# First pair's keys in two loads of 64 and 192 tiles instead of three, and the queries' load written with a leading dimension of two

## The chip, the cores and the metric

The kernel runs on one core of one Trainium2 chip. The metric is the device time of one execution in microseconds; a median of several runs is given, and one further execution was taken with the hardware profiler. Names of engines: PE is TensorE (PEld its weight loads), DVE is VectorE, ACT is ScalarE, POOL is GpSimd, SP is SyncE, which here only issues loads.

## The reference

One step of attention decoding with grouped queries: 32 query heads share 8 key and value heads, the context is 65,536 long, a head has 128 elements, all in bf16.

```python
B, Hq, Hkv, Sq, Sk, D = 1, 32, 8, 1, 65536, 128
...
k = jnp.repeat(k, rep, axis=1)
v = jnp.repeat(v, rep, axis=1)
scale = D ** -0.5
scores = jnp.einsum("bhqd,bhkd->bhqk", q, k) * scale
p = _softmax(scores, axis=-1)
return jnp.einsum("bhqk,bhkd->bhqd", p, v)
```

Keys and values are 134.2 MB each and are read once.

## The kernel before

Each of the 8 heads' context is cut into two halves, which makes 16 pairs of units ("pairs"). A pair has 256 tiles; a tile is 128 keys (one per partition) by 128 elements, so a pair's keys are 64 KB in each of the 128 partitions, and its values as many. The buffer `kbuf` holds a pair and 96 tiles more, `vbuf` one pair.

**TensorE** runs one loop over the pairs (`tensor_engine`, L223). Before the keys of pair i it takes the values of pair i-1 (`pe_values`). In the first round there are none, and it transposes the queries instead (`pe_queries`, L217): it waits for `q_sem`, which the queries' load raises, and for the identity matrix, makes one transpose at L220, and waits until DVE has copied the result. Then come the keys (`pe_keys`, L164): groups of eight tiles are transposed into PSUM (`pe_transposes`, the matmul at L139), evicted to `ktb` by DVE (L245) or ACT (L243), and multiplied with the head's queries (`pe_scores`, L157) eight groups later. The first 20 groups (160 tiles) form the first unit of the pair, the last 12 (96 tiles) the second. The code of the last 12 groups stands twice, behind an If each, for even and odd pairs.

**What the keys' loads promise.** `K_PARTS = (0, 64, 160)` gives the tiles at which TensorE takes a semaphore: `krdy[0]` ahead of tile 0, `krdy[1]` ahead of tile 64 (group 8), `krdy[2]` ahead of tile 152 (group 19, the last of the first unit). `load_k(i, odd, split)` makes one load for each entry of `split`: a load that begins at part f and reaches to the next entry raises `krdy[f]` by 16 when it has landed, and the semaphores of the parts that it swallows are raised by SP itself, right after the issue. Most pairs are loaded in one piece, the first in three.

**SP** (`sync_engine`, L457) issues, in this order: pair 0's keys, pair 0's values, then for every further pair its keys after `kfree` and its values after `vfree`. `kfree` is raised by DVE and ACT when the group 19 of the pair before is in PSUM (L241), `vfree` by DVE when the pair's value products are done (L326). All these loads run on one queue, in the order of issue. The last pair's values come in pieces, so that little work is left when the last has landed.

**ACT** issues the queries' load as its first instruction (L428): 32 rows of 128 elements into 32 partitions. It is on ACT's own queue, beside the keys.

DVE, ACT and POOL also make the softmax: maxima, exponentials and their sums for a unit of 160 and one of 96 tiles, and the rescaling of the running output.

Of the kernel before, what the change touches and what calls it, by code (L numbers as in the profile page):

```python
# [41 lines left out]
def take(e, sem, n=1):  # L42

    e.wait_ge(sem, n)
    e.sem_inc(sem, -n)  # L45


def bass_standalone__gqa_softmax__decode_kernel(nc, q, k, v, out):
# [14 lines left out]
    def row_tile(odd, x):  # L63
        return (x + C) % (2 * T) if odd else x

    kf, vf, qf, of = k[0], v[0], q[0, :, 0, :], out[0, :, 0, :]
# [4 lines left out]
    def sb(name, shape, dt):  # L71
        return S(nc.sbuf_tensor(name, shape, dt))

    def sem(name):
        return S(nc.semaphore(name))
# [5 lines left out]
    qsb = sb("qsb", [HR, D], DT.bfloat16)  # L81
# [42 lines left out]
    q_sem, o_sem, s_x, t_z, t_id, t_if, t_qT = (  # L124
        sem(n) for n in ("q_sem", "o_sem", "s_x", "t_z", "t_id", "t_if", "t_qT"))
# [294 lines left out]
    def act_round(e, i):  # L420
        for j in range(G):
            if on_act(j):
                evict(e, j)
        exponentials(e, 2 * i)
        exponentials(e, 2 * i + 1)

    def scalar_engine(e):
        e.dma_start(qsb[:, :], qf).then_inc(q_sem, 16)  # L428
        e.wait_ge(t_z, 1)
        e.activation(dscr[:, 1:2], dscr[:, 0:1], AF.Exp, scale=1.0)  # L430
        with e.Fori(0, H):
            for i in range(HALVES):
                act_round(e, i)
        e.wait_ge(t_row, 1)
        e.dma_start(of[0:HR - R, :], orow[R:HR, :]).then_inc(o_sem, 16)
# [17 lines left out]
    def pairs(x):  # L453

        return x.rearrange("h (c p t) d -> (h c) p (t d)", c=HALVES, p=P)

    def sync_engine(e):  # L457
        kp, vp = pairs(kf), pairs(vf)

        def cols(a, b):  # L460
            return slice(a * D, b * D)

        def load_k(i, odd, split=(0,)):

            for n, f in enumerate(split):
                last = (split + (len(K_PARTS),))[n + 1]
                a, b = K_PARTS[f], (K_PARTS + (2 * T,))[last]
                r = row_tile(odd, a) if b - a < 2 * T else 0
                t = r if odd else C + r
                e.dma_start(kbuf[:, cols(t, t + b - a)], kp[i][:, cols(r, r + b - a)]).then_inc(krdy[f], 16)  # L470
                for x in range(f + 1, last):
                    e.sem_inc(krdy[x], 16)

        def load_v(i, ready, a, b):
            e.dma_start(vbuf[:, cols(a, b)], vp[i][:, cols(a, b)]).then_inc(ready, 16)

        def load_both(i, odd):
            take(e, kfree)
            load_k(i, odd)
            take(e, vfree)  # L480
            load_v(i, vrdy[0], 0, 2 * T)
            e.sem_inc(vrdy[1], 16)

        load_k(0, 0, (0, 1, 2))
        load_v(0, vrdy[0], 0, 2 * T)

        for sm in [vrdy[1]] + vpiece:
            e.sem_inc(sm, 16)
        load_both(1, 1)
        with e.Fori(1, H - 1) as h:  # L490
            load_both(2 * h, 0)
            load_both(2 * h + 1, 1)
        i = NR - 2
        take(e, kfree)
        load_k(i, 0, (0, 2))
        take(e, vfree)
        load_v(i, vrdy[0], 0, A)
        load_v(i, vrdy[1], A, 2 * T)
        i = NR - 1
        take(e, kfree)  # L500
        load_k(i, 1, (0, 1, 2))
        take(e, vfree)
        for sm in vpiece:
            e.sem_inc(sm, -16)
        load_v(i, vrdy[0], C, 2 * T)
        e.sem_inc(vrdy[1], 16)
        r = 0
        for n, sm in zip(V_PIECES, vpiece):
            load_v(i, sm, r, r + n)
            r += n  # L510
        ins = e.dma_start(of[HR - R:HR, :], olast[:, :])
        ins.wait_op(t_last, 1, "sem-ge")
        ins.then_inc(o_sem, 16)


    tensor_engine(nc.tensor)
    vector_engine(nc.vector)
    scalar_engine(nc.scalar)
    gpsimd_engine(nc.gpsimd)
    sync_engine(nc.sync)  # L520
    nc.sync.wait_ge(o_sem, 32)
    es.close()
# [27 lines left out]
```

## Time and profile before

| | us |
|---|---|
| median of 3 runs (lowest, highest) | 628.41 (628.28, 628.63) |
| span of the profiled execution | 627.2 |
| PE busy | 489.5 (78%) |
| DVE busy | 284.8 (45%) |
| ACT busy | 235.2 (37%) |
| q1, SP's queue: data moved | 268.44 MB |
| rate over the span | 428 GB/s |

The span runs from the first to the last instruction of the profiled execution; the runs' times also hold what lies around it. In the page's rows of forty slices, one slice is 15.7 us, and each digit is a busy share in tenths. "DMA" there is the mean over the core's 16 DMA engines. A row of the timeline gives start, duration, engine, line, operation, what is written and what read, the count, and in brackets how long the engine was idle before and what ended that; "issue" means that the profile shows nothing it waited for. A row of a DMA queue gives packets, MB and the packets' time as a share of 16 engines over the window; the packets of a short window are put to the window in which they begin, so a share there can be over 100%. Queue q1 is SP's, q10 ACT's, and q8 brings instructions. A load's row of packets consists of one packet per partition and a small one of 4 bytes per engine that reports the end.

### The profile page before, as it was taken

To read this page: it belongs to the slowest core of one execution; us is meant where nothing else is said; L and a number is where in the kernel's file an instruction comes from. 1 tells how busy PE (TensorE), PEld (TensorE's weight loads), DVE (VectorE), ACT (ScalarE), POOL (GpSimd) and SP (SyncE) were. 2 spreads that over 40 slices of the span, in tenths; PEclk is the share of its full clock that TensorE was granted. 3 is DMA by queue.
4 is the path that set the end of the run, shared out by engine and by line. 5 is a ranking of instruction groups with operands and counts; after the bars stand their busy time and mean duration, and the time that the engine had idled before them with its cause. 6 is when DMAs were issued, how large, how long until landed. Compare 5 with 4: busy or idle time off the path is not lost. (4 is left out here: it accounts for less than half of the span.)

```text
span 627.2 us, 27059 instructions
## 1 busy us (share of the span) xinstructions
PE 489.5 (78%) x12290; PEld 485.2 (77%) x12290; DVE 284.8 (45%) x667; ACT 235.2 (37%) x466; POOL 16.4 (3%) x49
## 2 busy tenths in 40 slices
PE   1773995949959497696976949779595896999897
PEld 1773995949859497696976949779595896989896
DVE  2531553615536164351644516345172452747264
ACT  1430442504425053251533605335152351535253
POOL 0000000000000000000000000000000000000000
PEclk9975886958869597685977959779596785969596
DMA  9999999999999999999999999999999999999997
GB/s 366 441 442 431 435 435 430 439 430 439 418 447 418 447 422 435 435 430 435 435 435 430 439 422 443 426 439 426 443 426 443 422 447 422 423 428 429 427 439 308
DMA packets 6155, 268.59 MB, mean 428 GB/s; under 512 B 770, under 2 KB 898, under 8 KB 1154
## 3 DMA queue, kind: packets, MB, share of 16 engines
q1 hardware_dynamic: 6056, 268.44, 99.2%
q8 instruction: 7, 0.11, 0.1%
q10 hardware_dynamic: 90, 0.02, 0.0%
q14 instruction: 2, 0.02, 0.0%
HBM read 268.44 MB, written 0.01 MB: 428 GB/s over the span
## 5 line engine op out<-in xcount | busy, mean ns | idle before, releaser
L139 PE MATMUL trb<-ident,kbuf 128*128 128x128 bf16 x4096 | 302.7, 237 | 107.0 <-PEq L45 100.4
L139 PEld LDWEIGHTS trb<-ident,kbuf 128*128 128x128 bf16 x4096 | 270.8, 107 | 108.5 <-issue 108.2
L243 ACT ACTIVATE ktb<-trb 128x1024 bf16<-128x1024 bf16 x176 | 180.1, 1023 | 350.6 <-PE trb L139 344.2
L245 DVE COPY ktb<-trb 128x1024 bf16<-128x1024 bf16 x336 | 222.0, 689 | 167.1 <-PE trb L139 164.0
L157 PE MATMUL qkb<-qcur,ktb 128*128 128x4 bf16 x4096 | 132.0, 164 | 0.0
L157 PEld LDWEIGHTS qkb<-qcur,ktb 128*128 128x128 bf16 x4096 | 124.1, 96 | 0.0
L183 PE MATMUL pvb<-pts,vbuf 128*128 128x4 bf16 x2560 | 71.6, 165 | 12.7 <-PEq L45 12.7
L183 PEld LDWEIGHTS pvb<-pts,vbuf 128*128 128x128 bf16 x2560 | 69.8, 101 | 14.6 <-issue 14.6
L413 ACT ACTIVATE pts<-qkb,negm 128x160 bf16<-128x160 f32 (+1 forms) x128 | 51.9, 548 | 0.0
L280 DVE TENSOR_REDUCE cmax<-qkb 128x4 f32<-128x640 f32 (+1 forms) x32 | 22.1, 691 | 59.6 <-DVEq L45 59.6
L183 PE MATMUL qkb<-pts,vbuf 128*128 128x4 bf16 x1536 | 43.3, 166 | 4.6 <-PEq L45 4.6
L183 PEld LDWEIGHTS qkb<-pts,vbuf 128*128 128x128 bf16 x1536 | 42.4, 104 | 5.1 <-issue 5.0
L413 ACT ACTIVATION_READ_ACCUMULATOR pts<-qkb,negm 128x1 f32 x128 | 34.2, 267 | 0.0
L449 POOL PARTITION_ALL_REDUCE cmaxa<-cmax x32 | 12.0, 374 | 576.5 <-POOLq L45 576.5
L407 ACT ACTIVATE alpha<-dm 128x4 f32<-128x4 f32 x32 | 6.4, 201 | 32.0 <-ACTq L45 32.0
L330 DVE COPY acc<-qkb 128x4 f32<-128x4 f32 x8 | 1.3, 162 | 35.2 <-DVEq L45 35.2
L308 DVE TENSOR_TENSOR lp<-lp,alpha 128x4 f32<-128x4 f32 x24 | 3.9, 163 | 26.9 <-DVEq L45 26.9
L319 DVE TENSOR_TENSOR acc<-acc,pvb 128x4 f32<-128x4 f32 x32 | 5.1, 158 | 22.6 <-DVEq L45 21.8
L220 PE MATMUL trb<-ident,qsb 32*128 32x32 bf16 x1 | 0.2, 178 | 11.7 <-issue 11.7
L220 PEld LDWEIGHTS trb<-ident,qsb 32*128 32x128 bf16 x1 | 0.1, 100 | 11.6 <-issue 11.6
L297 DVE TENSOR_TENSOR m<-m,cmaxa 128x4 f32<-128x4 f32 x24 | 3.8, 160 | 8.8 <-DVEq L45 8.8
L316 DVE TENSOR_TENSOR acc<-acc,alpha 128x4 f32<-128x4 f32 x24 | 3.9, 162 | 4.2 <-DVEq L45 3.7
(42 smaller groups left out, 37.6 us busy)
## 6 DMA issues: line engine op xcount, KB each, us to landing
kbuf<-in_k_dram SPq DMA_DIRECT2D x5, 3072.0 KB, 24.6
vbuf<-in_v_dram SPq DMA_DIRECT2D x2, 5120.0 KB, 23.2
kbuf<-in_k_dram SPq DMA_DIRECT2D x1, 5120.0 KB, 17.8
kbuf<-in_k_dram SPq DMA_DIRECT2D x2, 2048.0 KB, 13.4
vbuf<-in_v_dram SPq DMA_DIRECT2D x1, 3072.0 KB, 26.9
vbuf<-in_v_dram SPq DMA_DIRECT2D x1, 1984.0 KB, 30.8
vbuf<-in_v_dram SPq DMA_DIRECT2D x1, 704.0 KB, 32.1
vbuf<-in_v_dram SPq DMA_DIRECT2D x1, 288.0 KB, 32.4
```

Source lines behind the costliest of these rows:

```text
L139: ins = pe.transpose(trb[j % NTB][:, i * P:(i + 1) * P], kbuf[:, t * D:(t + 1) * D], ident[:, :])
L157: ins = pe.matmul(bank[:, t * R:(t + 1) * R], lhsT=ktb[:, off:off + P], rhs=qcur[:, :], start=True, stop=True)
L183: ins = pe.matmul(vsum[q], lhsT=vbuf[:, r * D:(r + 1) * D], rhs=pts[:, r * R:(r + 1) * R], start=r == a, stop=r == b - 1)
L243: ins = e.activation(dst, trb[j % NTB][:, :], AF.Copy).then_inc(eva, 1)
L245: ins = e.tensor_copy(dst, trb[j % NTB][:, :]).then_inc(evd, 1)
L280: e.tensor_reduce(cmax[:, :], qkb[part][:, 0:n * R].rearrange("p (t g) -> p g t", g=R), AX.X, ALU.max).then_inc(cm, 1)
L308: chain(e, lambda: e.tensor_tensor(lp[:, :], lp[:, :], alpha[u % 2][:, :], ALU.mult), lambda: e.tensor_tensor(lp[:, :], lp[:, :], rsum[u % ...
L316: return lambda: e.tensor_tensor(acc, acc, alpha[u % 2][:, :], ALU.mult)
L319: return lambda: e.tensor_tensor(acc, acc, vsum[q], ALU.add)
L407: e.activation(alpha[u % 2][:, :], dm[u % 2][:, :], AF.Exp, scale=scale)
L413: ins = e.activation(pv[:, g, r:r + n], sv[:, g, 0:n], AF.Exp, bias=negm[b][:, g:g + 1], scale=scale, accum_out=rsum[b][:, g:g + 1])
L449: e.partition_all_reduce(cmaxa[:, :], cmax[:, :], P, bass.bass_isa.ReduceOp.max).then_inc(cma, 1)
```

## The change

```diff
     def scalar_engine(e):
-        e.dma_start(qsb[:, :], qf).then_inc(q_sem, 16)
+        e.dma_start(qsb[:, :], qf.rearrange("(a b) d -> a b d", a=2)).then_inc(q_sem, 16)
...
-        load_k(0, 0, (0, 1, 2))
+        load_k(0, 0, (0, 1))
         load_v(0, vrdy[0], 0, 2 * T)
```

The first pair's keys are loaded in two pieces: tiles 0 to 63 as before, and tiles 64 to 255 in one load, which raises `krdy[1]`; SP raises `krdy[2]` itself behind it. The queries' source is written as two blocks of 16 rows.

On SP, at the start of the program, the difference between the orders of the two kernels is this (a row is a load with its destination's partitions and elements):

```order
 L470 DMA kbuf<-in_k_dram 128x8192
-L470 DMA kbuf<-in_k_dram 128x12288 x2
+L470 DMA kbuf<-in_k_dram 128x24576
 L475 DMA vbuf<-in_v_dram 128x32768
 L470 DMA kbuf<-in_k_dram 128x32768
```

Two loads of 96 tiles have become one of 192; the loads around it stand as before.

On ACT, at the start, the changed kernel's order reads so; `qsb` takes the queries, `dscr` is a scratch tile, `ktb` the evicted keys:

```order
L428 DMA qsb<-in_q_dram 32x128
L430 ACT_TABLE_LOAD
L430 ACTIVATE dscr<-dscr 128x1
L431 UNCONDITIONAL_BRANCH
```

These rows are the same in the kernel before, and nothing moved; on PE, DVE and POOL the orders are the same too.

On PE, at the start of the first round and then at the turn from tile 63 to tile 64, these are the rows with the semaphores that each waits for, the same in both kernels (`evd` and `eva` count evictions by DVE and ACT):

```order
L220 MATMUL trb<-ident,qsb 128x32 [waits t_id,q_sem]
L229 UNCONDITIONAL_BRANCH [waits t_qT]
L231 COMPARE_AND_BRANCH
L139 MATMUL trb<-ident,kbuf 128x128 [waits krdy0]
```

```order
L139 MATMUL trb<-ident,kbuf 128x128 [waits krdy1,eva]
L139 MATMUL trb<-ident,kbuf 128x128 x7
L157 MATMUL qkb<-qcur,ktb 128x4 [waits qrdy,evd]
L157 MATMUL qkb<-qcur,ktb 128x4 x7
L139 MATMUL trb<-ident,kbuf 128x128 [waits evd]
```

No row moved here, but `krdy1` now stands for all of the pair's remaining tiles, and the queries' transpose (`q_sem`) still comes ahead of the first keys.

## Prediction

> **What bounds the kernel now.** I read the page first, for the DMA row and the queues.
>
> ```profile
> span 627.2 us, 27059 instructions
> ...
> DMA  9999999999999999999999999999999999999997
> ...
> q1 hardware_dynamic: 6056, 268.44, 99.2%
> q8 instruction: 7, 0.11, 0.1%
> q10 hardware_dynamic: 90, 0.02, 0.0%
> ```
>
> The DMA engines are busy in every slice but the last, and nearly all of it is q1, SP's queue of keys and values. So the time is the start of that stream, the stream, and what follows it. The next views are SP's part of the timeline (start, duration) and the DMA issues of short windows (size, us from issue to landing).
>
> ```profile
> 0.73 1.38 SPq L470 DMA_DIRECT2D kbuf<-in_k_dram  x3
> 2.15 1.54 SPq L475 DMA_DIRECT2D vbuf<-in_v_dram  x1
> 27.64 0.33 SPq L470 DMA_DIRECT2D kbuf<-in_k_dram  x1
> 54.01 0.33 SPq L475 DMA_DIRECT2D vbuf<-in_v_dram  x1
> ...
> 590.73 2.25 SPq L475 DMA_DIRECT2D vbuf<-in_v_dram  x5
> ```
>
> ```profile
> kbuf<-in_k_dram SPq DMA_DIRECT2D x1, 2048.0 KB, 8.4
> qsb<-in_q_dram ACTq DMA_DIRECT2D x1, 8.0 KB, 4.8
> kbuf<-in_k_dram SPq DMA_DIRECT2D x1, 3072.0 KB, 15.6
> kbuf<-in_k_dram SPq DMA_DIRECT2D x1, 3072.0 KB, 22.4
> vbuf<-in_v_dram SPq DMA_DIRECT2D x1, 41.3
> kbuf<-in_k_dram SPq DMA_DIRECT2D x1, 35.4
> vbuf<-in_v_dram SPq DMA_DIRECT2D x1, 96.0 KB, 32.1
> ```
>
> The three issues at 0.73 take 1.38 us, so they start near 0.7, 1.2 and 1.7, and the loads land near 9.1, 16.8 and 24.1. The queries, issued with them, land near 5.5. Pair 0's values land at 2.15 + 41.3 = 43.5 and pair 1's keys at 27.64 + 35.4 = 63.0: each load is issued many microseconds before the queue reaches it. The last 96 KB are issued near 592.6 and land near 624.7, 2.5 us before the span ends. So the first pair's work matters only if it makes a load that has to wait for it (pair 1's keys at 27.64, pair 1's values at 54.01) reach the queue after the queue has run dry. TensorE's timeline shows what they wait for.
>
> ```profile
> 11.66 0.18 PE L220 MATMUL trb<-ident,qsb 32*128 32x32 bf16 x1 [11.66 <-issue]
> 12.89 5.92 PE L139 MATMUL trb<-ident,kbuf 128*128 128x128 bf16 x72 [1.05 <-PEq L45]
> ...
> 26.93 0.56 PE L139 MATMUL trb<-ident,kbuf 128*128 128x128 bf16 x7 [1.39 <-issue]
> ...
> 34.47 8.38 PE L139 MATMUL trb<-ident,kbuf 128*128 128x128 bf16 x96 [5.21 <-issue]
> ...
> 63.13 1.12 PE L139 MATMUL trb<-ident,kbuf 128*128 128x128 bf16 x9 [9.37 <-PEq L45]
> ```
>
> TensorE ends pair 0 and then idles 9.37 us until pair 1's keys have landed. That idle time is the cover for everything that gets later before it. The three earlier gaps, ended by "issue", have no data wait that fits: the queries are there at 5.5 and all keys at 24.1. The instruction queue fits:
>
> ```profile
> q8 instruction: 1, 0.02, 63.4%
> q8 instruction: 1, 0.02, 32.0%
> ```
>
> These are q8's packets in the windows 24.5 to 24.6 and 31.8 to 32.0, each some 2.5 us ahead of a resumption of TensorE (26.93, 34.47). I read the gaps as waits for code, which shares the DMA engines with the keys.
>
> **The change part by part.** Packet sizes come first: q1 in the windows 5 to 7 (packets of 16 KB), 9 to 14 (24 KB) and 64 to 80 (64 KB).
>
> ```profile
> q1 hardware_dynamic: 51, 0.84, 97.4%
> q1 hardware_dynamic: 88, 2.16, 101.0%
> q1 hardware_dynamic: 112, 7.08, 102.9%
> ```
>
> Share times 16 engines times window, over packets: 0.61 us for 16 KB, 0.92 us for 24 KB; the third row's 7.08 MB are 108 packets of 64 KB, 2.44 us each. On the line between the ends 48 KB take 1.83 us.
>
> *The stream.* Two loads of 96 tiles become one of 192: on each engine eight packets of 1.83 us replace sixteen of 0.92, which saves between 0 and 0.1 us; I take 0.05. SP issues one load less (about 0.4 us) and reaches the values sooner; the queue is far behind, so that is worth nothing. The third semaphore is now added by SP at once; TensorE takes it only after the second, so it guards nothing and delays nothing.
>
> *The wait for the second part.* Tile 64 now waits for all 256 tiles. In the row at 12.89, 64 of 72 transposes are done near 18.2; the wait now ends where the third load landed, at 24.1. TensorE is **5.9 us** later there. Everything behind it on its queue waits with it: the remaining transposes and scores, so the evictions, the release of kbuf and the release of vbuf.
>
> *Slow restart.* After an idle stretch TensorE starts slowly. Two rows of the busy time by stage:
>
> ```profile
> 14.00:16.00 2.00, 2.00 (x22) 2.00 (x20) 0.98 (x2) 1.02 (x1) 0.00 (x0) 1.00 1.08 451
> 20.00:22.00 2.00, 2.00 (x55) 2.00 (x53) 1.40 (x3) 1.02 (x1) 0.00 (x0) 1.00 1.29 557
> ```
>
> 22 matmuls per 2 us against 55; but the first are all transposes, the second half scores. An estimate for some 4 us of it in the mixed stretch is between 0 and 1.3 us; I take 0.6, in the middle.
>
> *Code.* The fetch of the piece used from 26.93 will queue behind value packets of 2.44 us. The stall of 1.39 us can vanish or grow by one packet: -1.4 to +2.4, taken as +0.5, since value packets were there at the end of the old wait too. The 5.21 us stall before 34.47 has already met those packets; it can only catch a better moment: -2.4 to 0, taken as -1.2. The fetch before 11.66 can now stand behind 1.83 instead of 0.92 us; that 0.9 lies ahead of the new wait and costs nothing.
>
> *What follows.* Pair 1's keys were issued at 27.64; now at 27.64 + 5.9 + 0.6 + 0.5 = 34.6, at worst 37.2. Values land at 43.5, so the queue does not run dry. Pair 1's values were issued at 54.01; the shift is 5.9 + 0.6 + 0.5 - 1.2 = 5.8, so 59.8, between 56.1 (5.9 - 1.4 - 2.4) and 63.6 (5.9 + 1.3 + 2.4). How late may they be? At the start, 15 packets are moving by 2.5 us (window 0.5 to 2.5), 1.8 us after the issue at 0.73; and the engines finish pair 1's keys spread out, ten of the 4-byte reports (under 512 B) before 62.05 and six after:
>
> ```profile
> q1 hardware_dynamic: 15, 0.25, 57.4%
> DMA packets 21, 0.72 MB, mean 352 GB/s; under 512 B 10, under 2 KB 10, under 8 KB 10
> DMA packets 15, 0.59 MB, mean 621 GB/s; under 512 B 6, under 2 KB 6, under 8 KB 6
> ```
>
> (windows 60 to 62.05 and 62.05 to 63). The last engines, which set the end, go on without a gap if the issue is before about 63.0 - 1.8 = 61.2. At 59.8 it is; the early engines may pause a little and lose only their lead. TensorE then ends pair 0 5.8 us later, inside its 9.37 us of idling, and starts pair 1 at 63.1 as before. From there nothing differs.
>
> *The queries.* The patterns in the built program are the same 32 rows of 128 on both sides: splitting contiguous rows in two is folded back, and ACT's order is unchanged. I cost it at nothing; the other case is a rival.
>
> *The sum.* 627.2 - 0.05 + 0 = 627.2 us of span. The runs' median is 628.41, 1.2 us more than the span of the profiled execution, which lies around it. Forecast **628.4 us**. A measurement of this kernel can tell about 0.2% (1.26 us) from no change.
>
> **The rivals.**
>
> *Two engines carry the queries after all (chance 0.10; slower).* The place is L220. In the window 2.9 to 4.22 the two queues took turns, one packet each:
>
> ```profile
> q1 hardware_dynamic: 31, 0.51, 95.0%
> q10 hardware_dynamic: 31, 0.01, 2.7%
> ```
>
> Two engines would carry 16 rows and a report each, 17 turns: eight end with the 16-KB packets near 7.4, one falls between the loads, eight go by at 1.83 us, so the queries land near 7.4 + 14.6 + 0.4 = 22.4 instead of 5.5. TensorE would start at 22.4 instead of 11.66, a shift of 10.7 in place of 5.9 and 0.6; with -0.7 for the code, pair 1's values are issued near 64.0, 2.8 us past 61.2: **631.2**, between 628.4 (code at -3.8) and 634.3 (code at +2.4). It decides once the queries land past about 19 (7.2 + 0.7 behind 11.66). Against it: q10's 90 packets of before are what 16 engines for this load would give (32 rows and 16 reports, the rest output), and the built pattern has not changed. [...]
>
> *Pair 1's values come late (0.12; level to slower).* The same mechanism with the keys alone, if the restart and the code fetches go badly: beyond a shift of 7.2 each microsecond costs one, up to 63.6 - 61.2 = 2.4: **628.4 to 630.8**. For it: two of my terms have bounds wider than the margin of 1.4 us. Against: they would have to go badly together. Of the 0.12 about 0.05 lie over 0.2%.
>
> *The removed load had a fixed cost on the path (0.02; faster).* The first load lands 8.4 us after its issue, of which eight packets of 0.61 are 4.9; if the other 3.5 stood in the queue at each load, one load less would give 628.4 - 3.5 = **624.9**. Against: the second and third loads land 7.3 us apart, exactly eight packets of 0.92. [...]
>
> **How the numbers follow.** Forecast 0.76 (628.0 to 628.9), late values 0.12, queries 0.10, fixed cost 0.02. Within 0.2% are 0.76 and 0.07 of the late values: 0.83. Slower are 0.10 + 0.05 = 0.15, faster 0.02. The range 627.9 to 630.0 holds the forecast and most of the late values, and leaves the queries' case and the gain outside.
>
> **What would show it.** Right: the queries transposed near 11.7 to 12.6, a gap before tile 64 that ends near 24.1, pair 1's values issued near 60, its transposes at 63.1, the DMA row full. Wrong: 17 packets in a row of turns on q10 and L220 past 20 us; pair 1's transposes later than 64; a slice near 62 us with less DMA; or a changed last stage.

## The result and the profile after

| | median | lowest to highest | runs |
|---|---|---|---|
| before | 628.36 us | 628.09 to 628.63 | 21 |
| after | 629.69 us | 628.26 to 632.32 | 21 |

The ratio is 1.002 (95% interval 1.0015 to 1.0026): slower, by a little over 1 us. (The ratios here and below are worked out from the single runs, none of them in the slow state, and need not equal the quotient of two medians.) What the medians hide is the spread: 0.5 us before, 4 us after. The fastest run after, 628.26 us, is as fast as those before.

The page of the changed kernel, the same rows as before:

```profile
span 628.9 us, 27059 instructions
...
DMA  9999999999999999999999999999999999999996
...
q1 hardware_dynamic: 5912, 268.44, 99.0%
q8 instruction: 7, 0.11, 0.1%
q10 hardware_dynamic: 90, 0.02, 0.0%
```

SP's queue has 144 packets fewer, 128 rows and 16 reports: one load less. ACT's queue has 90 as before, 48 of them before 6 us in either kernel: the queries' 32 rows and still 16 reports. SP's part of the timeline:

```profile
0.73 0.89 SPq L470 DMA_DIRECT2D kbuf<-in_k_dram  x2
1.73 0.37 SPq L475 DMA_DIRECT2D vbuf<-in_v_dram  x1
34.64 0.33 SPq L470 DMA_DIRECT2D kbuf<-in_k_dram  x1
60.90 0.33 SPq L475 DMA_DIRECT2D vbuf<-in_v_dram  x1
76.93 0.34 SPq L470 DMA_DIRECT2D kbuf<-in_k_dram  x1
...
594.84 2.23 SPq L475 DMA_DIRECT2D vbuf<-in_v_dram  x5
```

Pair 1's keys are issued 7.0 us later than before (34.64 for 27.64) and its values 6.9 us later (60.90 for 54.01). The next load, at 76.93, stands where it stood. TensorE's rows say where the 7 us come from:

```profile
10.59 0.18 PE L220 MATMUL trb<-ident,qsb 32*128 32x32 bf16 x1 [10.59 <-issue]
11.82 5.98 PE L139 MATMUL trb<-ident,kbuf 128*128 128x128 bf16 x64 [1.05 <-PEq L45]
23.96 1.01 PE L139 MATMUL trb<-ident,kbuf 128*128 128x128 bf16 x8 [6.16 <-PEq L45]
...
33.59 0.91 PE L139 MATMUL trb<-ident,kbuf 128*128 128x128 bf16 x8
34.33 1.94 PE L157 MATMUL qkb<-qcur,ktb 128*128 128x4 bf16 x72
41.46 8.29 PE L139 MATMUL trb<-ident,kbuf 128*128 128x128 bf16 x96 [5.18 <-issue]
...
63.12 6.38 PE L139 MATMUL trb<-ident,kbuf 128*128 128x128 bf16 x72 [2.48 <-PEq L45]
```

They show the wait at tile 64 (6.16 us), the slow groups after it, no stall any more at tile 153, the same 5.2 us stall before the last 96 tiles, and then an idle time of 2.48 us in place of 9.37 ahead of pair 1, which starts at 63.1 as before. So TensorE has caught up at 63.1, and yet the span is 1.7 us longer. The time is lost on the queue. A load of a pair is 128 packets of 64 KB. I count eight for each of the 16 engines that report: eight packets of 2.42 us are 19.4 us, and one such load lands 19.3 us behind the other in the kernel before (63.0 and 82.3). First the packets of q1 in the changed kernel, in the windows 61.84 to 62.50 (five of the 19 are reports) and 62.60 to 64.00:

```profile
q1 hardware_dynamic: 19, 0.92, 410.1%
q1 hardware_dynamic: 2, 0.13, 30.4%
```

and, in the kernel before, the window 61.80 to 62.60 (eight of the 16 are reports):

```profile
q1 hardware_dynamic: 16, 0.52, 152.0%
```

Share times 16 times the window over the packets of 64 KB: before, the last eight engines go over to pair 1's values with packets of 2.43 us. After, 14 engines begin the values between 0.9 and 1.6 us after the issue, and their first packets take 3.09 us on average; two begin later still, near 63.2 and 63.5, with 3.40 us on average. The last first packet thus ends near 66.8, in the kernel before near 64.9. The delay is still there at the end of the stream (issues of the changed kernel, us to landing):

```profile
kbuf<-in_k_dram SPq DMA_DIRECT2D x1, 6144.0 KB, 22.6
vbuf<-in_v_dram SPq DMA_DIRECT2D x1, 23.1
vbuf<-in_v_dram SPq DMA_DIRECT2D x1, 96.0 KB, 29.7
```

The merged load of keys lands near 1.3 + 22.6 = 23.9, with the old third load. Pair 1's values land at 60.90 + 23.1 = 84.0, against 54.01 + 28.3 = 82.3 in the kernel before (its row is shown below). The last piece lands near 596.7 + 29.7 = 626.4, against 624.7: the 1.7 us lost near 62 are the 1.7 us of the span.

### The profile page after: what moved, and what is told of

Read it like the earlier page. It is cut to its first block, busy times and chain, and to the rows that moved or that the text cites. A ratio compares the mean times of both kernels' runs of the same rounds, so it can differ in the third digit from the quotient of the medians.

```text
span 628.9 us, 27059 instructions
## 1 busy us (share of the span) xinstructions
PE 488.1 (78%) x12290; PEld 483.9 (77%) x12290; DVE 284.0 (45%) x667; ACT 235.4 (37%) x466; POOL 16.5 (3%) x49
## 5 line engine op out<-in xcount | busy, mean ns | idle before, releaser
L220 PE MATMUL trb<-ident,qsb 32*128 32x32 bf16 x1 | 0.2, 182 | 10.6 <-issue 10.6
L220 PEld LDWEIGHTS trb<-ident,qsb 32*128 32x128 bf16 x1 | 0.1, 99 | 10.6 <-issue 10.6
## 6 DMA issues: line engine op xcount, KB each, us to landing
kbuf<-in_k_dram SPq DMA_DIRECT2D x1, 6144.0 KB, 22.6
vbuf<-in_v_dram SPq DMA_DIRECT2D x1, 704.0 KB, 29.7
```

## The experiments

The theory, after the result: the later wait at tile 64 delays pair 0, that delays the issue of pair 1's values, and these come when the queue is running dry. Rivals: the queries' load; the merged load as such (packets of 48 KB, one load less); TensorE's slower first pair in some other way.

### The two edits apart, and the wait without the merged load

e1, the keys' edit alone:

```diff
-        load_k(0, 0, (0, 1, 2))
+        load_k(0, 0, (0, 1))
```

> Theory (late values): the keys' two loads alone carry the whole effect. The first pair's chain ends about 7 us later, pair 1's values are issued near 61 instead of 54, just as the queue runs dry, and the median comes out like the changed kernel's, 629 to 630.5 us, with single runs scattered from 628.3 to 632. Rival (the queries' rewritten load costs the time): no change from the kernel before, 628.4 us within 0.3.

e2, the queries' edit alone:

```diff
-        e.dma_start(qsb[:, :], qf).then_inc(q_sem, 16)
+        e.dma_start(qsb[:, :], qf.rearrange("(a b) d -> a b d", a=2)).then_inc(q_sem, 16)
```

> Theory (late values): the rewritten queries' load is the same load; 628.4 us within 0.3, single runs as close together as the kernel before, 16 reports of 4 bytes on ACT's queue. Rival (the queries' load runs on two engines or costs the time): 629 us or more, two reports instead of sixteen, the queries' transpose past 20 us.

e3, three loads, the last part ahead of the middle one (`end` is a new argument that bounds the last part):

```diff
-        load_k(0, 0, (0, 1, 2))
+        load_k(0, 0, (0,), 1)
+        load_k(0, 0, (2,))
+        load_k(0, 0, (1,), 2)
```

> Three loads as in the kernel before, with the same packets of 24 KB, but tiles 160 to 255 are loaded ahead of tiles 64 to 159, so tile 64 waits until all is there. Theory (the later wait is what costs, through pair 1's values): values issued near 61, time like the changed kernel's, 629 to 630.5 us, scattered. Rival (the load of 192 tiles with its packets of 48 KB, or one load less, is what costs): 628.4 us within 0.3.

e4, one load:

```diff
-        load_k(0, 0, (0, 1, 2))
+        load_k(0, 0, (0,))
```

> All 256 tiles in one load: tile 0 waits until 24 us. Theory (late values): the first pair's chain starts 12 to 13 us later than before (24 for 11.7), with a slow restart and the code stalls where they were; pair 1's keys are issued near 40 and its values near 66 to 67, 5 to 6 us past the end of its keys in the queue: 633 to 636 us. Rival (the size or the number of the loads costs, not the wait): at most 2 us over the kernel before, 628 to 630.5.

| | median (lowest to highest) | before, same chip | ratio (95%) |
|---|---|---|---|
| e1 keys only | 630.52 (629.66 to 633.1) | 628.3 | 1.0043 (1.0029 to 1.0056) |
| e2 queries only | 628.32 (628.24 to 628.45) | 628.3 | 1.0 (0.9992 to 1.0009) |
| e3 last part first | 630.57 (628.53 to 633.05) | 628.3 | 1.0031 (1.0019 to 1.0043) |
| e4 one load | 631.85 (631.6 to 632.43) | 628.3 | 1.0058 (1.0045 to 1.0071) |

The queries' edit does nothing. Its page has the queue row of before:

```profile
q10 hardware_dynamic: 90, 0.02, 0.0%
```

The keys' edit does all, and e3 shows that it is the wait: with three loads and the old packets, only in an order that makes tile 64 wait, the time is lost and scatters in the same way. Two things stay open here: e1 loses more than the changed kernel (1.0029 to 1.0056 against 1.0015 to 1.0026), in a series of six runs, and no run tells why; and in the traced execution of e3 some 1.4 us more go at a later load (pair 5's values land 20.8 us after its keys, where 19.3 to 19.4 is the rule). The issue of pair 1's values in the timelines of e1, e3 and e4:

```profile
60.69 0.33 SPq L475 DMA_DIRECT2D vbuf<-in_v_dram  x1
```

```profile
61.08 0.33 SPq L475 DMA_DIRECT2D vbuf<-in_v_dram  x1
```

```profile
63.45 0.33 SPq L475 DMA_DIRECT2D vbuf<-in_v_dram  x1
```

e4 was expected at 633 to 636 us with an issue near 66 to 67; it came out at 631.85 and 63.45. The mechanism held, my chain was too long: TensorE waits once, and from there meets no second wait and no slow groups with scores between them (its groups take 0.61 us from 29.76 on; its first row then):

```profile
24.04 5.68 PE L139 MATMUL trb<-ident,kbuf 128*128 128x128 bf16 x72 [10.86 <-PEq L45]
```

### The issue late, and nothing else

The first attempt put reductions over a scratch tile on DVE ahead of the release of `vbuf`, for the first head:

```diff
         take(e, pvd, 2)
+        if i == 0:
+            with e.If(h < 1):
+                for n in range(6):
+                    e.tensor_reduce(padm[:, n * R:(n + 1) * R], pad[:, :].rearrange("p (t g) -> p g t", g=R),
+                                    AX.X, ALU.max)
         e.sem_inc(vfree, 1)
```

> The kernel before, with four reductions over a scratch tile on DVE (some 0.8 us each, first head only) ahead of the release of vbuf by pair 0; nothing else is delayed. Theory (late values): pair 1's values issued near 57 instead of 54, ahead of the queue's end at 61 to 63: 628.3 us within 0.3, single runs close together. Rival (TensorE's slower first pair costs, not the issue): 628.3 too.

> As the run with four, with six reductions. Theory (late values): issued near 59, still ahead of the first engine's end near 60.7 less the 1.0 us from issue to first packet: 628.3 to 628.8 us. Rival (TensorE's slower first pair costs): 628.3 within 0.3.

> As before, with eight reductions. Theory (late values): issued near 60.6 to 61, like the changed kernel's 60.9 while TensorE's pair 0 and pair 1's keys stay early: 629 to 631 us and scattered over 2 us or more. Rival (TensorE's slower first pair costs): 628.3 within 0.3, close together.

> As before, with eleven reductions. Theory (late values): issued near 63 to 63.5, with all engines idle, like the kernel with one load (63.45): 631.5 to 632 us and close together. Rival (TensorE's slower first pair costs): 628.3 within 0.3.

Medians: e5 628.41 us, e6 628.39, e7 628.68 (628.52 to 628.9), e8 630.68 (628.51 to 633.32), against 628.34 before on the same chip; ratios 1.0001, 1.0001, 1.0005 and 1.0032, the first three with intervals that hold 1, e8's 1.0016 to 1.0048. They are no test of the issue, since it did not move. e6's timeline, SP and DVE:

```profile
54.18 0.33 SPq L483 DMA_DIRECT2D vbuf<-in_v_dram  x1
```

```profile
53.89 7.17 DVE L331 TENSOR_REDUCE padm<-pad 128x4 f32<-128x640 f32 x6 [4.63 <-DVEq L45]
```

The semaphore instruction of its own did not wait for the reductions queued before it: the load it releases is issued at 54.18, and they run until 61.06. What the reductions did delay, as I read it, are DVE's evictions of pair 1, and in e8 another load is late, pair 2's keys:

```profile
79.65 0.34 SPq L478 DMA_DIRECT2D kbuf<-in_k_dram  x1
```

That is 76.94 in the kernel before; the values ahead of it in the queue, issued at 54 as ever, land at 82.1. Pair 2's keys land 22.5 us after them, against 19.4 in the kernel before. So e8 is the same loss at another load, which I had not planned.

The second attempt lets the last reduction raise the semaphore:

```diff
+                    ins = e.tensor_reduce(...)
+                ins.then_inc(vfree, 1)
+            with e.If(h > 0):
+                e.sem_inc(vfree, 1)
```

> The kernel before; now the last of the reductions on DVE itself raises the semaphore (first head only), so that the issue of pair 1's values waits for all of them (in the runs e5 to e8 it did not: it stayed at 54). Five reductions of 1.19 us: issued near 59.6, first packets near 60.6, as the first engine runs out. Theory (late values): 628.3 to 629 us, little scatter. Rival (TensorE's slower first pair costs): 628.3 within 0.3.

> As the run with five, with six: issued near 60.8, as in the changed kernel (60.9), while TensorE's first pair and pair 1's keys stay early. Theory (late values): 629 to 631 us, single runs scattered over 2 us or more. Rival (TensorE's slower first pair costs): 628.3 within 0.3, close together.

> As the run with five, with eight: issued near 63.1, when every engine has run out, as in the kernel with one load (63.45). Theory (late values): 631.3 to 632 us, close together. Rival (TensorE's slower first pair costs): 628.3 within 0.3.

> As e9 to e11, with four reductions: issued near 58.5, first packets near 59.5, 1.1 us before the first engine has run out at 60.6. Theory (a late issue costs only when an engine has run out before its first packet is there): 628.3 to 628.6 us, close together. Rival (the engines need the next load's packets longer ahead, 2 us or more before the end): 629 to 631 us.

| issue of pair 1's values, traced execution | kernel | median (lowest to highest) | ratio (95%) |
|---|---|---|---|
| 54.01 | before | 628.36 (628.09 to 628.63) | |
| 58.71 | e15, four | 628.48 (628.27 to 629.26) | 1.0003 (0.9994 to 1.0012) |
| 59.79 | e9, five | 630.98 (630.5 to 633.01) | 1.0048 (1.0035 to 1.0061) |
| 60.89 | e10, six | 630.74 (630.21 to 632.95) | 1.0037 (1.0024 to 1.005) |
| 63.35 | e11, eight | 631.94 (630.49 to 632.21) | 1.0052 (1.0039 to 1.0065) |

The rows of e15, e9, e10 and e11 from which the first column is taken:

```profile
58.71 0.33 SPq L487 DMA_DIRECT2D vbuf<-in_v_dram  x1
```

```profile
59.79 0.33 SPq L487 DMA_DIRECT2D vbuf<-in_v_dram  x1
```

```profile
60.89 0.33 SPq L487 DMA_DIRECT2D vbuf<-in_v_dram  x1
```

```profile
63.35 0.33 SPq L487 DMA_DIRECT2D vbuf<-in_v_dram  x1
```

In e10 TensorE's pair 0 and all keys are early; it sits idle as long as before ahead of pair 1:

```profile
62.91 5.85 PE L141 MATMUL trb<-ident,kbuf 128*128 128x128 bf16 x72 [9.52 <-PEq L45]
```

So the issue alone makes the loss, and the rival of TensorE's slow first pair falls. e6 and e7 are the control: the same six and eight reductions as in e10 and e11, with the issue left near 54, give 628.39 and 628.68 us where e10 and e11 give 630.74 and 631.94.

By the medians the edge is between 58.7 and 59.8. The first engine ends pair 1's keys near 60.4 (the first report of these traces begins between 60.3 and 60.6), so that is between 1.7 and 0.6 us ahead of it. I had expected e9 to cost little; it costs as much as e10. But a median and the one issue that was traced are not of the same execution: e15's traced execution is the slowest of its eleven (629.26 us). The traces themselves say more. These are the issue rows of pair 1's values, us to landing, of the kernel before, e12 (described below), e15, e9, e1, e10, e3, e11 and e4:

```profile
vbuf<-in_v_dram SPq DMA_DIRECT2D x1, 28.3
vbuf<-in_v_dram SPq DMA_DIRECT2D x1, 24.7
vbuf<-in_v_dram SPq DMA_DIRECT2D x1, 24.2
vbuf<-in_v_dram SPq DMA_DIRECT2D x1, 24.2
vbuf<-in_v_dram SPq DMA_DIRECT2D x1, 22.8
vbuf<-in_v_dram SPq DMA_DIRECT2D x1, 24.0
vbuf<-in_v_dram SPq DMA_DIRECT2D x1, 24.3
vbuf<-in_v_dram SPq DMA_DIRECT2D x1, 21.7
vbuf<-in_v_dram SPq DMA_DIRECT2D x1, 22.0
```

and these, one packet each, the first packet of the values that ends last: e15 in the window 61.5 to 61.6, e9 in 63.1 to 63.4, e10 in 63.8 to 64.0, e3 in 64.2 to 64.4:

```profile
q1 hardware_dynamic: 1, 0.07, 255.7%
q1 hardware_dynamic: 1, 0.07, 71.9%
q1 hardware_dynamic: 1, 0.07, 114.6%
q1 hardware_dynamic: 1, 0.07, 121.2%
```

That is 4.09, 3.45, 3.67 and 3.88 us for a packet that takes 2.43 in the kernel before. In the table, the third column is the end of the last of the 16 first packets, found in windows of 0.1 us or less.

| traced execution | issue | last first packet ends | values land | span |
|---|---|---|---|---|
| before | 54.01 | 64.9 | 82.3 | 627.2 |
| e12 | 57.43 | 64.7 | 82.1 | 627.6 |
| e15 | 58.71 | 65.6 | 82.9 | 627.9 |
| e9 | 59.79 | 66.7 | 84.0 | 629.6 |
| e1 | 60.69 | 66.2 | 83.5 | 628.3 |
| e10 | 60.89 | 67.6 | 84.9 | 631.4 |
| after | 60.90 | 66.8 | 84.0 | 628.9 |
| e3 | 61.08 | 68.2 | 85.4 | 631.7 |
| e11 | 63.35 | 67.9 | 85.0 | 630.2 |
| e4 | 63.45 | 68.2 | 85.5 | 630.5 |

In every row the load lands 17.1 to 17.4 us after the third column; its seven further packets of 2.42 us are 16.9 of them. So, as I read these rows, what a late issue costs at this load is set by the one engine whose first packet ends last: it begins late, up to 3.5 us after the issue (e9), or takes long, up to 4.09 us (e15), or both. Against the 82.3 of the kernel before, the values land no later with the issue at 57.43, 0.6 us later at 58.71, 1.2 to 3.1 us later from 59.79 to 61.08, and 2.7 and 3.2 us later near 63.4. At nearly the same issue, 60.69 to 61.08, the delay differs by 1.9 us. In e10 and e3 a further 1.6 and 1.4 us go at later loads.

### The time given back

e12 exchanges the two Ifs that hold the last twelve groups, in the changed kernel:

```diff
-        with pe.If(i % 2 > 0):
-            for j in range(GA, G):
-                pe_transposes(pe, j, j * TB - A)
         with pe.If(i % 2 < 1):
             for j in range(GA, G):
                 pe_transposes(pe, j, C + j * TB)
+        with pe.If(i % 2 > 0):
+            for j in range(GA, G):
+                pe_transposes(pe, j, j * TB - A)
```

> The changed kernel with the two copies of the last twelve groups in the other order, so that the first pair finds half of its copy in code that is already there. Theory (late values, with the code stall of 5.2 us as a term of the delay): the stall shrinks by 2 to 4 us, pair 1's values are issued near 57 to 59 and the time goes back to 628.3 to 628.7 us with little scatter, although the keys still come in two loads. Rival (the two loads cost in some other way): as the changed kernel, 629.7.

e13 leaves that alone and splits pair 1's values in the changed kernel; DVE reports pair 0's first products apart (`vfirst`, which SP waits for):

```diff
-        take(e, pvd, 2)
+        if i:
+            take(e, pvd, 2)
+        else:
+            take(e, pvd)
+            e.sem_inc(vfirst, 1)
+            take(e, pvd)
...
-        load_both(1, 1)
+        take(e, kfree)
+        load_k(1, 1)
+        e.wait_ge(vfirst, 1)
+        load_v(1, vrdy[0], 0, A)
+        take(e, vfree)
+        load_v(1, vrdy[1], A, 2 * T)
```

> The changed kernel, but pair 1's values come in two loads, and the first, of 160 tiles, is issued as soon as pair 0's products of these tiles are done, some 3 us ahead of the rest: near 57.8 instead of 60.9; the rest stays near 60.9, behind 12 us of queue. Theory (late values): the loss goes: 628.3 to 628.8 us, close together, with TensorE's first pair as late as in the changed kernel. Rival (the two loads of keys, or TensorE's slow first pair, cost in some other way): 629.7 and scattered, as the changed kernel.

e14 is the exchange in the kernel before, e16 the changed kernel with both the exchange and the split.

> The kernel before with the two copies of the last twelve groups exchanged. If the exchange itself costs (in pair 1, whose copy is now the farther one): 629 to 631 us, scattered like e12, by a late issue of a later load. If it does not: 628.3 within 0.3, and e12's miss stays open.

> The changed kernel with both: the copies exchanged as in e12, and pair 1's values in two loads, the first issued early, as in e13. If e12's loss is that of pair 1's values in its other executions: 628.3 within 0.3, close together. Rival (another load, such as pair 1's own successor, runs late when the copies are exchanged): 629 to 631 us, scattered.

| | median (lowest to highest) | ratio (95%) |
|---|---|---|
| e12 exchange | 630.88 (628.32 to 631.7) | 1.0037 (1.0024 to 1.0049) |
| e13 values in two | 628.32 (628.19 to 628.59) | 1.0 (0.9991 to 1.0009) |
| e14 exchange, kernel before | 628.32 (628.17 to 629.06) | 1.0002 (0.9993 to 1.0011) |
| e16 exchange, values in two | 628.31 (628.17 to 628.96) | 1.0 (0.9991 to 1.0009) |

e13 settles it from the other side. Its keys come in two loads and TensorE's first pair is as late as in the changed kernel (its rows for SP and for TensorE's last 96 tiles); only the first of the two value loads is issued earlier:

```profile
34.61 0.33 SPq L475 DMA_DIRECT2D kbuf<-in_k_dram  x1
57.58 3.46 SPq L480 DMA_DIRECT2D vbuf<-in_v_dram  x2
```

```profile
41.53 8.00 PE L139 MATMUL trb<-ident,kbuf 128*128 128x128 bf16 x96 [5.29 <-issue]
```

The loss and the scatter are gone (628.19 to 628.59 us). The second load's issue, near 60.7, is no later than the changed kernel's, but it stands behind 160 tiles of queue.

e12 missed: its profiled execution (629.0 us) issues the values at 57.43 and loses nothing in that stretch, but its other runs have a median above 630. e14 and e16 say that the exchange costs nothing by itself and that e12's loss, too, is that of pair 1's values. The rows of e12 and e16, whose TensorE programs are the same, show how much that moment moves from one execution to another: in e16 the second load is issued when e12's only one would be, near 56.66 + 3.46 - 0.33 = 59.8.

```profile
57.43 0.33 SPq L475 DMA_DIRECT2D vbuf<-in_v_dram  x1
```

```profile
56.66 3.46 SPq L480 DMA_DIRECT2D vbuf<-in_v_dram  x2
```

One is ahead of the edge, the other beyond it. That e12's slower runs were those beyond it is argued from this, not seen. None of these kernels beats the kernel before by more than the interval.

## Why the prediction was wrong

The forecast was no change, 628.4 us in a range of 627.9 to 630.0. The median lies in that range; the direction did not: the loss is clear of the noise, though hardly larger than what I called measurable. The nearest case was the second rival, to which I gave 0.12; but it, too, charged nothing for a shift below 7.2 us, and the shift was 6.9, so that its range holds the result is luck.

- **What bounds the kernel**: right. The stream decides, and the first pair matters only through the issues at 27.64 and 54.01. Pair 1 starts at 63.1 in both.
- **The stream, one load less**: right to the extent that it shows: e13, with the merged load, is level with the kernel before.
- **The wait at tile 64**: 5.9 us forecast; 23.96 against 18.2, so 5.8.
- **Slow restart**: mis-sized. I took 0.6 and allowed 1.3. From tile 64 to the scores at 34.33 are 10.37 us; in the kernel before, from 18.2 to the scores at 27.33, 9.13 with 1.39 of stall, so 7.74 of work: it cost 2.6 us. Two rows of the busy time by stage of the changed kernel, with the granted clock in the third column from the end:

```profile
26.00:28.00 2.00, 2.00 (x34) 2.00 (x32) 0.69 (x1) 0.85 (x1) 0.00 (x0) 0.50 1.06 459
32.00:34.00 2.00, 1.87 (x48) 1.73 (x46) 1.40 (x3) 1.02 (x1) 0.00 (x0) 1.00 0.77 328
```

  Six groups ran at half the clock and took 1.06 us each (the next group's row begins at 25.03 after 23.96) in place of 0.65. My 4 us of slow time were too few and my gain per group too small. In this trace the granted clock is at 0.50 from 20.0 on, 2.2 us after the last transpose before the wait (17.8), and the return took 6.4 us: the restart is at 23.96, and the clock is at 1.00 from 30.35 on, where the first group of 0.61 us begins.

```profile
30.35 0.61 PE L139 MATMUL trb<-ident,kbuf 128*128 128x128 bf16 x8
```

- **Code**: the first stall vanished in this execution (-1.4, the lower bound, where I took +0.5; in e1's, with the same keys' loads, 0.86 us of it stayed); the second stayed at 5.18 (the upper bound, where I took -1.2). Together -1.4 for -0.7. That these stalls are waits for code is my reading; in e12, with the copies exchanged, the first 48 of the last 96 transposes begin at 34.59 with no stall, and one of 4.13 us stands ahead of their scores.
- **The sum of the shift**: 5.8 + 2.6 - 1.4 + 0 = 7.0, measured 6.9; forecast 5.8. An error of a microsecond, in a place with a margin of 1.4.
- **The deadline** is the step that failed. I put it at 61.2, by the last engine's end less the 1.8 us from an issue to the packets in motion, and priced what lies beyond at one microsecond each. The changed kernel is at 60.90, ahead of that, and loses 1.3 us in the median; in its trace the values land 1.7 us late. By e15 and e9 the medians turn between 58.7 and 59.8, so my own 59.8 would have been on the wrong side too. Three things were wrong. The 63.0 is the landing of the keys, while all 16 reports had begun by 62.6 (the row of the kernel before, above). The 1.8 us were those of 15 engines, and the last engine decides: my own row of the program's start has 15 packets, none begins between 2.5 and 2.9, so the sixteenth engine began at least 2.2 us after the issue at 0.73, and in the table above the last first packets begin 2.5 to 3.5 us after the issue where the queue had partly run dry (e9, e1, e10, after, e3). And I took a late load's first packet at its usual length: the same row gives 1.22 us for packets of 16 KB that I priced at 0.61 (57.4% of 16 engines over 2 us, over 15 packets), and a late load's first packets of 64 KB took 3.09 us on average, up to 4.09 (e15), in place of 2.43. I let early engines that run out lose only their lead, and the others go on unharmed; instead, one late and slow first packet delays the whole load.
- **The queries**: right that the built load is the old one (e2, 90 packets; L220 at 10.59 in the changed kernel). That a source in two blocks of rows could put the load on two engines was a supposition; no run shows it, and the changed kernel's load has 16 reports and lands 4.4 us after its issue.
- **The fixed cost of a load**: right that it does not stand in the queue: one load less brings nothing that shows (e13, ratio 1.0).

What stays open: why the first packets of a load that comes too late are slow and some of them late, and which engines these are, since the records of packets do not name their engine. The scatter of the changed kernel can have two sources, both seen in the traces: an issue that moves by some 2 us between executions (e12, e16) and a last first packet that differs at the same issue (e1, e10, after, e3); the runs without a profile do not show the share of each.

## What to carry to other kernels

This kernel lives from one queue, and the issue of pair 1's values had a deadline, which is not the moment at which the last engine runs out but lies earlier, before the first one does. An issue about 3 us ahead of the first engine's end lost nothing in its trace (e12), one 1.8 us ahead lost 0.6 us (e15), and one 0.6 us ahead 1.7 us (e9); later ones lost 1.2 to 3.2 us, which depended more on the slowest first packet than on the lateness. So judge a change of the start by the least slack of any later load, take the term with the widest bounds to its bad end, count the last engine and not most of them, and look at the spread of the runs: in e15 it grew to 1.0 us while the median stayed level. Where the slack is short, splitting the next load so that its first part can be issued from what is already free cost nothing here and took the loss away (e13).

## What the runs showed that I had not expected

- In the changed kernel's trace the load issued as the queue ran dry had first packets of 64 KB of 3.09 us on 14 engines and 3.40 on two (means), against 2.43 in the kernel before, whose queue never ran dry; in ten traces the whole load landed 17.1 to 17.4 us after the last of its first packets.
- A semaphore instruction on DVE ran ahead of the reductions before it: `vbuf` was released and the load issued at 54.18 while they ran from 53.89 to 61.06 (e6).
- In two executions with the same TensorE program, pair 1's values became due at 57.4 and at 59.8 (e12, e16).
